# Attention and a feed-forward product on one core: VectorE's and GpSimd's two-operand SBUF operations planned apart, the softmax constant as an immediate

## The chip, the cores and the metric

The kernel runs on one core of one Trainium2 chip. The metric is device time in microseconds of one execution. TensorE (PE) multiplies matrices, with its weight loads (PEld) beside them; VectorE (DVE), ScalarE (ACT) and GpSimd (POOL) work on elements; SyncE (SP) issues nearly all DMAs. SBUF is the memory on the chip from which all of them read, PSUM the one into which PE writes its sums.

## The reference

```python
def _attn_ref(q, k, v):                     # q, k, v: 8 x 8 x 576 x 64
    ...
    scores = scale * np.matmul(q, k.transpose(0, 1, 3, 2))
    mask_local = (rel >= 0) & (rel < stride)              # stride 32, heads 0 to 3
    mask_strided = (rel >= 0) & (pos[None, :] % stride == pos[:, None] % stride)
    ...
    scores = scores - np.max(scores, axis=-1, keepdims=True)
    attn = np.exp(scores)
    attn = attn / (np.sum(attn, axis=-1, keepdims=True) + 1e-09)
    return np.matmul(attn, v).astype(np.float32)

def _moe_ref(x, w_in, w_out):               # x: 4608 x 512, w_in: 512 x 2048, w_out: 2048 x 512
    h = x @ w_in
    relu6 = np.clip(h + 3.0, 0.0, 6.0)
    g = h * relu6 / 6.0
    return (g @ w_out).astype(np.float32)
```

The output of the attention, heads side by side, is the x of the feed-forward part. All of it is float32.

## The kernel before

**Numbers in two parts.** A float32 operand of a large product is split into a high part (rounded to the format that PE takes, fp32r) and a low part (the rest, by a subtraction), and each product is done as three: high by high, high by low, low by high. So every weight tile, every x and every g needs a copy or cast for the high part and a subtraction for the low one. For x these are L430 on ACT and L433 on DVE; for g L887 on ACT and L890 on POOL.

**Weights.** Each of the 32 weight tiles is loaded raw by SP (L303) and put together from its bits: ACT takes the upper (L311) and the lower bits (L315), DVE joins them (L319, tiles `fi` and `fo` from `rawi` and `rawo`), ACT or POOL copies the high part (L327, L329, into `wi` or `wo`), and POOL or DVE subtracts for the low part (L337).

**Attention.** For each batch and pair of heads: PE turns q and k or DVE transposes them (L512, L529), PE makes the scores in PSUM (L597, L608), ACT or DVE copies them out as `e` (L619, L621), DVE finds the maximum (L631, L634), POOL subtracts it (L653, L638), ACT takes the exponential (L656, L641), DVE the sum (L659, L645). `inverse` adds 1e-9 from the tile `eps` (L663) and takes the reciprocal (L664), both on DVE. POOL multiplies (L668, L649), DVE transposes (L702, L708, L713, tiles `at`, `atloc`, `atkept`), and PE multiplies by v (L402, L746, L771, L787) into `pv`, from which x is split. The last 64 tokens of each batch go to `left` (L419, L421).

**Feed-forward.** Three batches (0, 1 and 2) run by themselves: for each of 16 chunks of the inner dimension, PE makes `ph` (L921 to L923), ACT applies the shifted relu (L956, tile `u`), DVE the gate (L960), ACT and POOL split g, and PE adds the second product into `acc` (L854 to L856). The weights arrive during the first of these, so it runs beside the weights' unpacking and the next batch's attention. The other batches (3 and 4, 5 and 6, 7 and the left tokens) run in three pairs, each with seven products of half size (L1094 to L1096) in place of eight, for which sums and differences of weights (L974, L984, L995, sent to memory and loaded again) and of x (L1033 and L1039, tiles `xc` and `hxf`) are made ahead, and results are put together from PSUM and the SBUF tile `htmp` (L1105, L1113). There the gate reads either `ph` in PSUM or `htmp` in SBUF.

**What sets the order.** No engine chooses at run time. Every operation is recorded in a `Plan` by `op`, with an engine (or several that could do it), a planned duration for each, what it reads and writes, and a due time. `emit` then goes through a simulated time: for each engine it takes the ready operation that can start first, by due time where several can, and of the engines the one whose operation starts earliest. The engine that gets it is fixed then, and each engine runs its operations in that order. An operation waits on its engine for those ahead of it whether it needs them or not. `emit` knows of DMA, of the fetch of PE's instructions, and of small matmuls that only fill PE's early gaps (`idle`); after 100 us of simulated time DVE waits `PATIENCE` (2 us) before it takes an operation that another engine could do too.

Of the kernel before, what the change touches and what calls it, by code (L numbers as in the profile page):

```python
# [20 lines left out]
P = 128  # L21
# [18 lines left out]
HIENG = {"ACT": 0.63, "POOL": 1.2}  # L40
# [22 lines left out]
PATIENCE = 2.0  # L63


class Plan:
# [12 lines left out]
    def op(self, engine, us, fn, reads=(), writes=(), due=0.0, room=0.0, mode="", after=0.0, take=None, give=None, early=0.0, words=6):  # L79
# [13 lines left out]
        self.ops.append((how, fn, before, due, room, mode, after, take, give, early, words))  # L93
        return n

    def emit(self, idle):
# [10 lines left out]
        mode, dma = "", 0.0  # L107
# [11 lines left out]
        while done < len(ops):  # L119
            done += 1  # L120
            best = None
            for e, r in ready.items():
                t0, first, kept = free[e], None, 0.0
                for due, n in sorted(r):
                    t = max(t0, avail[n] + (PATIENCE if e == "DVE" and avail[n] > WARM and len(ops[n][0]) > 1 else 0.0))
# [9 lines left out]
                if first is not None and (best is None or first[0] < best[0]):  # L135
                    best = (first[0], e, first[2])
            t, e, n = best
            how, fn, _, due, _, m, after, take, give, _, words = ops[n]
# [48 lines left out]
def attention_ffn(ctx: ExitStack, tc, q, k, v, w_in, w_out, out):  # L187
# [34 lines left out]
    eps = const.tile([P, 2, 8], F32, name="eps")  # L222
# [7 lines left out]
    def identity():  # L230
        nc.vector.memset(three, 3.0)
        nc.vector.memset(eps, 1.0e-9)
# [57 lines left out]
    def weight_part(k, w, g, i):  # L290
# [149 lines left out]
    def kept_pair(g):  # L440
# [220 lines left out]
        def inverse():  # L661
            x = st_of(1)
            nc.vector.tensor_tensor(out=x, in0=x, in1=eps[:n, :, :nblk], op=ALU.add)  # L663
# [5 lines left out]
        pool = 0.1 + 0.004 * cols  # L669
        red = 0.18 + 0.0019 * cols  # L670
        if shifted:
            for j in range(2):
                ej, sj = (ekey + "1", stkey + (1,)) if j else (ekey, stkey)
                op("DVE", 0.18 + 0.00095 * cols, partial(most_of, j), reads=[ej, stkey], writes=[sj], due=sd + 0.7)
                op("POOL", pool / 2 + 0.05, partial(less_of, j), reads=[sj], writes=[ej], due=sd + 1)
                op("ACT", 0.2 + 0.00085 * cols, partial(exp_of, j), writes=[ej], due=sd + 1.5)
        else:
            op("DVE", red, most, reads=[ekey, ekey + "1"], writes=[stkey], due=sd + 0.7)
            op("POOL", pool, less, reads=[stkey, ekey + "1"], writes=[ekey], due=sd + 1)
            op("ACT", 0.2 + 0.0017 * cols, exp, writes=[ekey], due=sd + 1.5)  # L680
        if shifted:
# [3 lines left out]
            for j in range(2):  # L685
                op("POOL", pool / 2 + 0.05, partial(norm_of, j), reads=[stkey], writes=[ekey + "1" if j else ekey], due=sd + 2.5)
        else:
            op("DVE", red, total, reads=[ekey, ekey + "1"], writes=[stkey], due=sd + 2)
            op("DVE", 0.4, inverse, writes=[stkey], due=sd + 2.1)
            op("POOL", pool, norm, reads=[stkey], writes=[ekey, ekey + "1"], due=sd + 2.5)  # L690
# [191 lines left out]
    def split_g(fc, uk, gk, due, t, held=False):  # L882
# [9 lines left out]
        op({"POOL": 1.35}, 0, lo, reads=[uk, gk[0]], writes=[gk[1]], due=due)  # L892
# [395 lines left out]
```

## Time and profile before

| | us |
|---|---|
| three runs | 929.01, 932.99, 928.42 |
| median | 929.01 |
| the profiled execution | 929.12 |
| its span, first to last instruction | 927.3 |
| PE busy in the span | 885.3 |

The mean granted clock of TensorE over the span is 0.978 of full speed. The page's slices show when each engine is busy: each digit is the share of a slice of 23.2 us in tenths.

```profile
PE   5789898999999999999999999999999999999997
DVE  3788866568766777466755723345457003323200
ACT  2656655333434435344444633444446234334421
POOL 3646765555765877222221955213139531112441
PEclk7579999999999999999999999999999999999999
```

PE is the engine that is nearly always busy; its gaps lie in the first slices. DVE, ACT and POOL are busiest in the first half, where softmax, the weights' unpacking and the sums for the pairs stand beside the products. A clock under 9 is in the first three slices.

### The profile page before, as it was taken

What the parts mean: (1) busy time and instruction counts of PE and PEld (TensorE: products, weight loads), DVE (VectorE), ACT (ScalarE), POOL (GpSimd) and SP (SyncE); (2) the same over time, 40 slices, a digit from 0 to 9 for tenths busy, and PEclk for the clock granted to TensorE, in tenths of its full rate; (3) what the DMA queues carried; (4) which work ended last, traced back from release to release, by engine and by line L of the source; (5) the groups of instructions that cost most, each with busy time, mean ns of one, the idle gap of its engine ahead of it and who ended that gap; (6) DMA issues with size and microseconds to landing.
All of it is one profiled execution on the core that took longest, in us unless ns stands there. A gap on an engine that the chain in (4) does not pass through costs nothing.

```text
span 927.3 us, 19470 instructions
## 1 busy us (share of the span) xinstructions
PE 885.3 (95%) x7747; PEld 711.9 (77%) x7747; DVE 488.8 (53%) x833; ACT 404.6 (44%) x736; POOL 428.6 (46%) x378
## 2 busy tenths in 40 slices
PE   5789898999999999999999999999999999999997
PEld 3668686776888788888788778888887887888786
DVE  3788866568766777466755723345457003323200
ACT  2656655333434435344444633444446234334421
POOL 3646765555765877222221955213139531112441
PEclk7579999999999999999999999999999999999999
DMA  9988999977688874799784687785745675555374
GB/s 161 236 251 206 249 236 333 282 177 190 181 197 242 209 189 112 205 260 230 218 209 149 194 257 196 238 210 192 227 156 211 200 236 185 194 192 188 120 213 137
DMA packets 229563, 191.71 MB, mean 207 GB/s; under 512 B 174944, under 2 KB 189280, under 8 KB 229472
## 3 DMA queue, kind: packets, MB, share of 16 engines
q1 hardware_dynamic: 226800, 189.35, 73.2%
q10 hardware_dynamic: 2672, 1.11, 0.6%
q8 instruction: 61, 1.00, 0.5%
q14 instruction: 30, 0.25, 0.1%
HBM read 157.91 MB, written 32.51 MB: 205 GB/s over the span
## 4 chain that ended last, share of the span: by engine, by line
PE 75%; POOL 6%; DMA 6%; DVE 5%; SPq 3%; issue 2%; ACT 2%; DVEq 0%; POOLq 0%; ACTq 0%
PE ph L1094 8%; PE ph L1095 7%; PE ph L1096 7%; PE acc L854 4%; PE acc L856 4%; PE acc L855 4%; PE ph L921 3%; PE ph L922 3%; PE ph L923 3%; PE ps L608 3%; DMA rawi<-in_moe_w_in_dram 3%; DMA qn<-in_q_dram 2%; POOL xc L1033 2%; PE acc2b L854 2%; PE acc2b L856 2%
## 5 line engine op out<-in xcount | busy, mean ns | idle before, releaser
L1113 DVE TENSOR_TENSOR htmp<-ph,htmp 128x512 f32<-128x512 f32 x72 | 49.7, 690 | 183.9 <-ACT htmp L1105 106.7
L1094 PE MATMUL ph<-xc,wi 128*128 128x512 f32 x336 | 133.4, 397 | 1.3 <-DVE htmp L1113 0.8
L1095 PE MATMUL ph<-xc,wi 128*128 128x512 f32 x336 | 131.1, 390 | 0.0
L1096 PE MATMUL ph<-xc,wi 128*128 128x512 f32 x336 | 130.9, 390 | 0.0
L890 POOL TENSOR_TENSOR g<-u,g 128x512 fp32r<-128x512 f32 x48 | 65.7, 1372 | 62.1 <-ACT g L887 50.1
L921 PE MATMUL ph<-x,wi 128*128 128x512 f32 x192 | 79.8, 415 | 7.9 <-DVE u L960 4.6
L922 PE MATMUL ph<-x,wi 128*128 128x512 f32 x192 | 76.8, 400 | 4.0 <-DVE x L433 2.6
L923 PE MATMUL ph<-x,wi 128*128 128x512 f32 x192 | 76.7, 399 | 0.8 <-POOL wi L337 0.8
L854 PE MATMUL acc<-wo,g 128*128 128x512 f32 x192 | 76.9, 401 | 0.0
L855 PE MATMUL acc<-wo,g 128*128 128x512 f32 x192 | 75.1, 391 | 1.5 <-issue 1.1
L1094 PEld LDWEIGHTS ph<-xc,wi 128*128 128x128 f32 x336 | 63.0, 188 | 17.2 <-DVE htmp L1113 2.0
L856 PE MATMUL acc<-wo,g 128*128 128x512 f32 x192 | 75.4, 392 | 0.2 <-POOL g L890 0.2
L1096 PEld LDWEIGHTS ph<-xc,wi 128*128 128x128 f32 x336 | 63.1, 188 | 13.4
L1095 PEld LDWEIGHTS ph<-xc,wi 128*128 128x128 f32 x336 | 63.1, 188 | 12.4
L708 DVE STREAM_TRANSPOSE atloc<-e 32x192 f32<-32x192 f32 x168 | 61.9, 369 | 15.9 <-POOL e L668 9.0
L1105 ACT COPY htmp<-ph 128x512 f32<-128x512 f32 x72 | 42.2, 587 | 50.0 <-PE ph L1096 48.1
L653 POOL TENSOR_TENSOR e<-e,st 128x288 f32<-128x288 f32 (+1 forms) x30 | 34.2, 1141 | 64.5 <-DVE st L631 64.4
L890 POOL TENSOR_TENSOR g12a<-u,g02a 128x512 fp32r<-128x512 f32 x16 | 20.6, 1289 | 83.4 <-ACT g02a L887 83.4
L956 ACT ACTIVATE u<-htmp,three 128x512 f32<-128x512 f32 x48 | 34.7, 723 | 44.5 <-DVE htmp L1113 44.5
L956 ACT ACTIVATE u<-ph,three 128x512 f32<-128x512 f32 x48 | 33.0, 688 | 44.2 <-PE ph L923 43.8
L960 DVE SCALAR_TENSOR_TENSOR u<-u,htmp 128x512 f32<-128x512 f32 x48 | 38.5, 802 | 22.9 <-ACT u L956 22.8
L890 POOL TENSOR_TENSOR g11a<-u,g01a 128x512 fp32r<-128x512 f32 x16 | 21.5, 1347 | 60.4 <-ACT g01a L887 52.2
(212 smaller groups left out, 2079.5 us busy)
## 6 DMA issues: line engine op xcount, KB each, us to landing
wo<-wod SPq DMA_DIRECT2D x128, 512.0 KB
wi<-wid SPq DMA_DIRECT2D x84, 512.0 KB
rawi<-in_moe_w_in_dram SPq DMA_DIRECT2D x16, 512.0 KB
rawo<-in_moe_w_out_dram SPq DMA_DIRECT2D x16, 512.0 KB
wod<-wo SPq DMA_DIRECT2D x16, 512.0 KB
wid<-st SPq DMA_DIRECT2D x64, 128.0 KB
qn<-in_q_dram SPq DMA_DIRECT2D x112, 72.0 KB
kn<-in_k_dram SPq DMA_DIRECT2D x112, 72.0 KB
```

What stands on the lines that cost most here:

```text
L708: nc.vector.transpose(at[PAD * (a + h):PAD * (a + h) + PAD, :, PAD * a:PAD * a + PAD], e[PAD * a:PAD * a + PAD, :, PAD * h:PAD * h + PAD])
L854: nc.tensor.matmul(acc, gh, woh, start=fc == 0, stop=False)
L855: nc.tensor.matmul(acc, gh, wol, start=False, stop=False)
L856: nc.tensor.matmul(acc, gl, woh, start=False, stop=end)
L890: on(e).tensor_tensor(out=to(1), in0=tiles[uk], in1=tiles[gk[0]].bitcast(F32), op=ALU.subtract)
L921: nc.tensor.matmul(ph, wih, xh, start=n_ == 0, stop=False)
L922: nc.tensor.matmul(ph, wih, xl, start=False, stop=False)
L923: nc.tensor.matmul(ph, wil, xh, start=False, stop=n_ == NCC - 1)
L956: nc.scalar.activation(make(), src(), AF.Relu, bias=three)
L1094: nc.tensor.matmul(ph, w[:, j, 0], x[:, 0], start=u in (0, 1, 3) and j == 0, stop=False, skip_group_check=u in (2, 4, 5, 6))
L1095: nc.tensor.matmul(ph, w[:, j, 0], x[:, 1], start=False, stop=False, skip_group_check=u in (2, 4, 5, 6))
L1096: nc.tensor.matmul(ph, w[:, j, 1], x[:, 0], start=False, stop=j == 1, skip_group_check=u in (2, 4, 5, 6))
```

## The change

An operation can be recorded with `port=True`. `emit` holds the time `port` at which the last such operation on DVE or POOL ends (less 0.13 us), and starts no further one on either before it. So the plan runs the marked operations of the two engines one after the other. Marked are the join of weight bits, the low part of weights, the softmax's subtraction and multiplication on POOL, the low part of g, the gate where it reads `htmp` (given by `give`), and the sums, differences and low parts for the pairs. Not marked are POOL's cast of the high part (L329), and DVE's low part of x, which reads PSUM.

DVE's 2 us of patience now hold only for unmarked operations; a marked one with a choice of engines goes at once. Where two engines could start at the same time, the one whose operation is due first comes first. Planned durations are set anew. And the sum's 1e-9 is added as an immediate (`tensor_scalar_add`), so that the tile `eps` and its memset go.

```diff
-HIENG = {"ACT": 0.63, "POOL": 1.2}
+HIENG = {"ACT": 0.63, "POOL": 0.62}
...
-PATIENCE = 2.0
+PATIENCE = {("DVE", False): 2.0, ("DVE", True): 0.0, ("POOL", True): 0.0}
+PORT = ("DVE", "POOL")
...
-                    t = max(t0, avail[n] + (PATIENCE if e == "DVE" and avail[n] > WARM and len(ops[n][0]) > 1 else 0.0))
+                    t = max(t0, avail[n] + (PATIENCE.get((e, ops[n][11]), 0.0) if avail[n] > WARM and len(ops[n][0]) > 1 else 0.0))
+                    if ops[n][11] and e in PORT:
+                        t = max(t, port)
...
-                if first is not None and (best is None or first[0] < best[0]):
-                    best = (first[0], e, first[2])
+                if first is not None and (best is None or first[:2] < best[3]):
+                    best = (first[0], e, first[2], first[:2])
...
+            if shared and e in PORT:
+                port = end - 0.13
...
-    eps = const.tile([P, 2, 8], F32, name="eps")
-        nc.vector.memset(eps, 1.0e-9)
...
-        op("DVE", 0.95, join, reads=[key], writes=[fkey], due=due - 3)
+        op("DVE", 0.69, join, reads=[key], writes=[fkey], due=due - 3, port=True)
-        op({"POOL": 1.4, "DVE": 0.75}, 0, lo, reads=[fkey, key], writes=[key + ("lo",), key], due=due - 1)
+        op({"POOL": 1.29, "DVE": 0.68}, 0, lo, reads=[fkey, key], writes=[key + ("lo",), key], due=due - 1, port=True)
...
-            nc.vector.tensor_tensor(out=x, in0=x, in1=eps[:n, :, :nblk], op=ALU.add)
+            nc.vector.tensor_scalar_add(x, x, 1.0e-9)
...
-        pool = 0.1 + 0.004 * cols
+        pool = 0.12 + 0.00355 * cols
...
-                op("POOL", pool / 2 + 0.05, partial(less_of, j), reads=[sj], writes=[ej], due=sd + 1)
+                op("POOL", pool / 2 + 0.05, partial(less_of, j), reads=[sj], writes=[ej], due=sd + 1, port=True)
...
-        op({"POOL": 1.35}, 0, lo, reads=[uk, gk[0]], writes=[gk[1]], due=due)
+        op({"POOL": 1.3}, 0, lo, reads=[uk, gk[0]], writes=[gk[1]], due=due, port=True)
...
-        op({"DVE": 0.69, "POOL": 1.4} if both else {"DVE": 0.69}, 0, gate, reads=reads, writes=[uk], give=give, due=due)
+        op({"DVE": 0.69, "POOL": 1.4} if both else {"DVE": 0.69}, 0, gate, reads=reads, writes=[uk], give=give, due=due, port=give is not None)
...
-                op({"POOL": 1.34, "DVE": 0.69}, 0, lo, reads=keys_of(*at), writes=[key(u)], due=due + 0.5 * j + 0.1 * u + 0.05)
+                op({"POOL": 1.3, "DVE": 0.69}, 0, lo, reads=keys_of(*at), writes=[key(u)], due=due + 0.5 * j + 0.1 * u + 0.05, port=True)
```

What an engine can do in place of another shifts too: POOL makes 20 of the 32 high parts of weights (16 before) and 25 of their low parts (22 before), DVE 15 of the 32 differences L984 (5 before) and 9 of the copies of scores out of PSUM (4 before). The lines of the file after the change stand three further on (L433 becomes L436), those of the weights' unpacking included.

The first place is DVE's order around the first batch's last x, the one for which PE stands still at 63.90 us. `x0_31` is the low part of x for the heads 6 and 7, made in two steps from two PSUM tiles `pv0_30` and `pv0_31`; `fi` and `fo` are joins, `wi` the low part of a weight. Before:

```order
L433 TENSOR_TENSOR x0_11_875<-pv0_11_811,x0_10_874 128x224
L319 SCALAR_TENSOR_TENSOR fo03_854<-fo03_854,rawo03_506 128x512
L319 SCALAR_TENSOR_TENSOR fi10_862<-fi10_862,rawi10_511 128x512
L319 SCALAR_TENSOR_TENSOR fi11_905<-fi11_905,rawi11_514 128x512
L433 TENSOR_TENSOR x0_31_941<-pv0_30_911,x0_30_940 128x4x4x16
L319 SCALAR_TENSOR_TENSOR fi12_931<-fi12_931,rawi12_520 128x512
L337 TENSOR_TENSOR wi10_944<-fi10_862,wi10_944 128x4x128
L433 TENSOR_TENSOR x0_31_941<-pv0_31_912,x0_30_940 128x4x4x16
L337 TENSOR_TENSOR wi12_963<-fi12_931,wi12_963 128x4x128
```

Now:

```order
L436 TENSOR_TENSOR x0_11_872<-pv0_11_810,x0_10_871 128x224
L322 SCALAR_TENSOR_TENSOR fi10_860<-fi10_860,rawi10_509 128x512
L322 SCALAR_TENSOR_TENSOR fi11_881<-fi11_881,rawi11_516 128x512
L322 SCALAR_TENSOR_TENSOR fi12_910<-fi12_910,rawi12_518 128x512
L340 TENSOR_TENSOR wi10_936<-fi10_860,wi10_936 128x4x128
L436 TENSOR_TENSOR x0_31_945<-pv0_30_912,x0_30_944 128x4x4x16
L424 COPY left3_86<-pv0_30_912 128x4x4x2
L340 TENSOR_TENSOR wi12_948<-fi12_910,wi12_948 128x4x128
L436 TENSOR_TENSOR x0_31_945<-pv0_31_913,x0_30_944 128x4x4x16
L322 SCALAR_TENSOR_TENSOR fi13_958<-fi13_958,rawi13_522 128x512
```

The join `fo03` is gone from here and the low part `wi10` has come ahead of the first step; between the two steps stand a copy to `left3` and a low part in place of a join and a low part.

The second place is DVE's order in the first batch's chunk 12, where PE waits at 149.11 us for the gate `u0_12`, which reads `ph` and so frees it for a next product. `st1_1` is a softmax sum, `atloc` are transposes (six each). Before:

```order
L663 TENSOR_TENSOR st1_1_1845<-st1_1_1845,eps_78 96x2x6
L664 RECIPROCAL st1_1_1845<-st1_1_1845 96x2x6
L319 SCALAR_TENSOR_TENSOR fi33_1923<-fi33_1923,rawi33_1350 128x512
L708 STREAM_TRANSPOSE atloc0_899<-e_98 32x6x32 x6
L708 STREAM_TRANSPOSE atloc1_907<-e_98 32x6x32 x6
L960 SCALAR_TENSOR_TENSOR u0_12_1982<-u0_12_1982,ph0_12_1873 128x512
L960 SCALAR_TENSOR_TENSOR u0_13_1994<-u0_13_1994,ph0_13_1917 128x512
L319 SCALAR_TENSOR_TENSOR fo30_1950<-fo30_1950,rawo30_1678 128x512
L319 SCALAR_TENSOR_TENSOR fo31_1999<-fo31_1999,rawo31_1568 128x512
```

Now:

```order
L666 TENSOR_SCALAR st1_1_1834<-st1_1_1834 96x2x6
L667 RECIPROCAL st1_1_1834<-st1_1_1834 96x2x6
L322 SCALAR_TENSOR_TENSOR fi32_1889<-fi32_1889,rawi32_1351 128x512
L532 STREAM_TRANSPOSE kplain_108<-kn2_2_1721 128x18x4x8
L340 TENSOR_TENSOR wi32_1914<-fi32_1889,wi32_1914 128x4x128
L711 STREAM_TRANSPOSE atloc0_905<-e_102 32x6x32 x6
L322 SCALAR_TENSOR_TENSOR fi33_1933<-fi33_1933,rawi33_1423 128x512
L711 STREAM_TRANSPOSE atloc1_931<-e_102 32x6x32 x6
L322 SCALAR_TENSOR_TENSOR fo30_1959<-fo30_1959,rawo30_1667 128x512
L963 SCALAR_TENSOR_TENSOR u0_12_1985<-u0_12_1985,ph0_12_1891 128x512
L963 SCALAR_TENSOR_TENSOR u0_13_2037<-u0_13_2037,ph0_13_1901 128x512
```

The two gates stood right behind the twelve transposes and ahead of the join `fo30`; now `fo30` comes ahead of them, and the low part `wi32` and the transpose `kplain` have come into the row ahead of the first six.

The third place is PE's order at the first pair's end, where PE waits at 531.61 us for `g10a_15`, the low part of the pair's last g. `ph1_` are products of the second pair, `acc0a_0` a sum of the first. Before:

```order
L1096 MATMUL ph1_0_0_6576<-xc1_0_6441,wi0_6435 128x512
L1094 MATMUL ph1_0_1_6584<-xc1_1_6454,wi0_6435 128x512
L1095 MATMUL ph1_0_1_6584<-xc1_1_6454,wi0_6435 128x512
L1096 MATMUL ph1_0_1_6584<-xc1_1_6454,wi0_6435 128x512
L854 MATMUL acc0a_0_5177<-wo15_6426,g00a_15_6573 128x512
L855 MATMUL acc0a_0_5177<-wo15_6426,g00a_15_6573 128x512
L856 MATMUL acc0a_0_5177<-wo15_6426,g10a_15_6590 128x512
```

Now:

```order
L1097 MATMUL ph1_0_0_6560<-xc1_2_6549,wi1_6469 128x512
L1098 MATMUL ph1_0_0_6560<-xc1_2_6549,wi1_6469 128x512
L1099 MATMUL ph1_0_0_6560<-xc1_2_6549,wi1_6469 128x512
L1097 MATMUL ph1_0_3_6615<-xc1_3_6475,wi1_6469 128x512
L1098 MATMUL ph1_0_3_6615<-xc1_3_6475,wi1_6469 128x512
L1099 MATMUL ph1_0_3_6615<-xc1_3_6475,wi1_6469 128x512
L1097 MATMUL ph1_0_3_6615<-xc1_3_6517,wi1_6469 128x512
L1098 MATMUL ph1_0_3_6615<-xc1_3_6517,wi1_6469 128x512
L1099 MATMUL ph1_0_3_6615<-xc1_3_6517,wi1_6469 128x512
L857 MATMUL acc0a_0_5174<-wo15_6425,g00a_15_6600 128x512
L858 MATMUL acc0a_0_5174<-wo15_6425,g00a_15_6600 128x512
L859 MATMUL acc0a_0_5174<-wo15_6425,g10a_15_6623 128x512
```

Nine matmuls of the second pair, which read `xc1_2` and `xc1_3`, stand now ahead of the sum that needs `g10a_15`, where before the sum came right after `ph1_0_1`.

More of the change, by code (lines that the diff above doesn't have):

```diff
@@ L77, in __init__, with op @@
         self.by = {}
-    def op(self, engine, us, fn, reads=(), writes=(), due=0.0, room=0.0, mode="", after=0.0, take=None, give=None, early=0.0, words=6):
+    def op(self, engine, us, fn, reads=(), writes=(), due=0.0, room=0.0, mode="", after=0.0, take=None, give=None, early=0.0, words=6, port=False):
         n = len(self.ops)
@@ L92, in op @@
         how = engine if isinstance(engine, dict) else {engine: us}
-        self.ops.append((how, fn, before, due, room, mode, after, take, give, early, words))
+        self.ops.append((how, fn, before, due, room, mode, after, take, give, early, words, port))
         return n
@@ L106, in emit @@
         slots = {}
-        mode, dma = "", 0.0
+        mode, dma, port = "", 0.0, 0.0
         held, turned = 0, 0.0
@@ L678, in kept_pair @@
             op("DVE", red, most, reads=[ekey, ekey + "1"], writes=[stkey], due=sd + 0.7)
-            op("POOL", pool, less, reads=[stkey, ekey + "1"], writes=[ekey], due=sd + 1)
+            op("POOL", pool, less, reads=[stkey, ekey + "1"], writes=[ekey], due=sd + 1, port=True)
             op("ACT", 0.2 + 0.0017 * cols, exp, writes=[ekey], due=sd + 1.5)
@@ L685, in kept_pair @@
             for j in range(2):
-                op("POOL", pool / 2 + 0.05, partial(norm_of, j), reads=[stkey], writes=[ekey + "1" if j else ekey], due=sd + 2.5)
+                op("POOL", pool / 2 + 0.05, partial(norm_of, j), reads=[stkey], writes=[ekey + "1" if j else ekey], due=sd + 2.5, port=True)
         else:
@@ L689, in kept_pair @@
             op("DVE", 0.4, inverse, writes=[stkey], due=sd + 2.1)
-            op("POOL", pool, norm, reads=[stkey], writes=[ekey, ekey + "1"], due=sd + 2.5)
+            op("POOL", pool, norm, reads=[stkey], writes=[ekey, ekey + "1"], due=sd + 2.5, port=True)
         vb = [slot(early) for _ in range(2)]
@@ L974, in whole @@
                     on(e).tensor_tensor(out=tiles[tk.key].rearrange("p (u x) -> p u x", u=FQ), in0=a, in1=d, op=ALU.add)
-                op({"POOL": 1.34, "DVE": 0.69}, 0, whole, reads=[key, key + ("lo",), "tmps"], writes=[tk], take=tk, due=due + kc, early=due)
+                op({"POOL": 1.3, "DVE": 0.69}, 0, whole, reads=[key, key + ("lo",), "tmps"], writes=[tk], take=tk, due=due + kc, early=due, port=True)
                 w.append(tk)
@@ L984, in mix @@
                     on(e).tensor_tensor(out=part(*to), in0=part(*a), in1=part(*d), op=how)
-                op({"POOL": 0.74, "DVE": 0.42}, 0, mix, reads=w, writes=[w[to[0]]], due=due + kc + 0.1)
+                op({"POOL": 0.74, "DVE": 0.42}, 0, mix, reads=w, writes=[w[to[0]]], due=due + kc + 0.1, port=True)
             for i, us in enumerate(((2, 3), (6, 4))):
@@ L1039, in go @@
                     on(e).tensor_tensor(out=src(*to), in0=src(*x), in1=src(*y), op=ALU.subtract)
-                op({"DVE": 0.69, "POOL": 1.34}, 0, go, reads=keys_of(*x) + keys_of(*y), writes=keys_of(*to), due=due + 0.5 * j)
+                op({"DVE": 0.69, "POOL": 1.34}, 0, go, reads=keys_of(*x) + keys_of(*y), writes=keys_of(*to), due=due + 0.5 * j, port=True)
             split(0, (0, 0))
```

6 lines of the change are left out of this document (3 added, 3 removed).

## The prediction

> **What bounds the kernel now.** I read the page's busy times first, then stretches of the span, then PE's waits, then the groups by form and the timeline around the largest waits.
>
> ```profile
> span 927.3 us, 19470 instructions
> PE 885.3 (95%) x7747; PEld 711.9 (77%) x7747; DVE 488.8 (53%) x833; ACT 404.6 (44%) x736; POOL 428.6 (46%) x378
> ```
>
> TensorE sets the end: it is busy for 885.3 of 927.3 us, so all its idle time is 42.0 us. The change takes no matmul away and shortens none. It can win only out of these 42 us, and out of time in which PE ran at a lowered clock. VectorE and GpSimd are half idle: what they gain in busy time is worth nothing by itself.
>
> ```profile
> 0.00:20.00 20.00, 13.21 (x221) 8.00 (x222) 8.76 (x17) 4.89 (x9) 7.23 (x30) 0.74 1.11 156
> 20.00:40.00 20.00, 14.17 (x244) 12.35 (x245) 13.73 (x35) 10.47 (x24) 12.06 (x13) 0.55 1.06 206
> 40.00:60.00 20.00, 16.31 (x286) 13.49 (x283) 15.27 (x36) 12.91 (x28) 12.47 (x16) 0.85 0.98 287
> 60.00:80.00 20.00, 17.37 (x187) 13.47 (x185) 16.45 (x20) 12.95 (x26) 11.06 (x10) 0.83 0.74 194
> 80.00:100.00 20.00, 20.00 (x233) 16.00 (x231) 15.39 (x26) 10.94 (x22) 11.51 (x10) 1.00 1.00 253
> 100.00:225.00 125.00, 114.42 (x1216) 89.56 (x1215) 90.45 (x160) 59.19 (x111) 73.94 (x61) 1.00 0.90 244
> 300.00:500.00 200.00, 199.78 (x2075) 161.08 (x2075) 134.62 (x241) 89.58 (x170) 88.38 (x74) 1.00 0.76 199
> 500.00:720.00 220.00, 215.50 (x1448) 174.66 (x1448) 105.40 (x151) 100.36 (x176) 102.96 (x76) 1.00 0.68 208
> ```
>
> Columns: stretch, its length, busy time of PE, PEld, DVE, ACT, POOL, the granted clock, the DMA share. PE idles 6.8, 5.8, 3.7 and 2.6 us in the first four stretches (18.9 together), 10.6 from 100 to 225, 4.5 from 500 to 720, and nearly nothing between. The clock is below full only in the first 80 us.
>
> ```profile
> PE qp L498 <- DMA qn<-in_q_dram: 5.2, 3, 2.5
> PE ps L608 <- issue: 5.1, 2, 4.3
> PE ph L921 <- DVE u L960: 4.6, 4, 2.2
> PE ph L921 <- POOL e L653: 3.2, 1, 3.2
> PE ph L922 <- DVE x L433: 2.6, 1, 2.6
> ...
> PE acc0a L856 <- POOL g10a L890: 1.5, 1, 1.5
> ...
> PE ps L597 <- DVE x L433: 1.4, 1, 1.4
> ...
> PE acc1a L856 <- POOL g11a L890: 1.2, 1, 1.2
> ...
> PE ph L923 <- POOL wi L337: 0.8, 1, 0.8
> PE acc1b L856 <- POOL g11b L890: 0.7, 1, 0.7
> ...
> PE acc L855 <- POOL wo L337: 0.5, 1, 0.5
> PE ph L1094 <- DVE g L960: 0.4, 1, 0.4
> ```
>
> These are PE's waits: total, count, longest. DMA (5.2) and issue (5.1) are out of this change's reach. Those that VectorE or GpSimd release can move: 4.6 + 2.6 + 1.5 + 1.4 + 1.2 + 0.8 + 0.7 + 0.5 + 0.4 = 13.7 us. I leave the 3.2 out: the timeline shows a fetch of PE's instructions inside that wait.
>
> **The exclusion of DVE and POOL is in the trace.**
>
> ```profile
> L960 DVE SCALAR_TENSOR_TENSOR u<-u,htmp 128x512 f32<-128x512 f32 x48 | 38.5, 802 | 22.9 <-ACT u L956 22.8
> L960 DVE SCALAR_TENSOR_TENSOR u<-u,ph 128x512 f32<-128x512 f32 x48 | 32.5, 679 | 19.0 <-ACT u L956 16.6 <-POOL htmp L984 2.1
> L1033 DVE TENSOR_TENSOR xc<-hxf,xc 128x512 fp32r<-128x512 f32 x15 | 21.4, 1427 | 1.9 <-ACT xc L1030 1.8
> L890 POOL TENSOR_TENSOR g11b<-g,g01b 128x512 fp32r<-128x512 f32 x16 | 20.6, 1290 | 17.6 <-ACT g01b L887 17.6
> ```
>
> ```profile
> 529.83 1.72 POOL L890 TENSOR_TENSOR g10a<-u,g00a 128x512 fp32r<-128x512 f32 x1
> ```
>
> The gate takes 679 ns with one operand in PSUM and 802 with both in SBUF; the low part L1033, both in SBUF, takes 1427 on DVE. POOL's low part of g takes 1290 in one form, and 1.72 us at the place where PE waits 1.5 for it. I read the stretched ones as held up by the other engine's operation; term 1 shows two of them side by side with it. By the Trainium skill, SBUF — State Buffer, section "Who interferes with whom", a DVE instruction with two SBUF inputs excludes a GpSimd instruction that reads SBUF, and the second waits out the first; these rows agree. The old plan did not know of it, so what it put side by side came late. The new plan starts no marked operation until the other engine's is done, with durations near these rows (1.30 on POOL, 0.69 on DVE). That, the tie between engines decided by due time, and the dropped patience of DVE change only the order; they go together in terms 1 to 3. From some 730 us on PE's rows are the same before and after, and SP's first 60 rows are too, so the first loads and the end stay as they are.
>
> **Term 1: the wait at 63.90 us.**
>
> ```profile
> 57.09 0.68 DVE L319 SCALAR_TENSOR_TENSOR fo<-fo,rawo 128x512 int32<-128x512 int32 x1
> ...
> 59.86 1.80 DVE L319 SCALAR_TENSOR_TENSOR fi<-fi,rawi 128x512 int32<-128x512 int32 x1
> 61.59 1.75 DVE L337 TENSOR_TENSOR wi<-fi,wi 128x512 fp32r<-128x512 f32 x1
> 63.26 0.58 DVE L433 TENSOR_TENSOR x<-pv,x 128x256 fp32r<-128x256 f32 x1
> ```
>
> ```profile
> 59.83 1.29 POOL L337 TENSOR_TENSOR wo<-fo,wo 128x512 fp32r<-128x512 f32 x1
> 61.07 1.71 POOL L337 TENSOR_TENSOR wi<-fi,wi 128x512 fp32r<-128x512 f32 x1
> ```
>
> ```profile
> 63.90 0.80 PE L922 MATMUL ph<-x,wi 128*128 128x512 f32 x1 [2.63 <-DVE x L433]
> ```
>
> The low part of x at 63.26 is what PE waits 2.63 us for. Ahead of it on DVE stand a join of 1.80 and a low part of 1.75, each while a POOL operation ran; the same join took 0.68 at 57.09. So 1.12 + 1.07 = 2.19 us of the wait is exclusion. The new order has as much ahead of it (three joins, two low parts and a copy, against four joins and a low part), but planned apart from POOL. Bounds: nothing to all 2.63; I take 2.0, near the 2.19.
>
> After that wait the clock falls: the stretch 60 to 80 is granted 0.83, a loss of 0.17 x 20 = 3.4 us. Bounds 0 to 3.4; a wait of 2.2 us from 100 to 225 left the clock at 1.00 there, so a rest of under 1 us should leave it too. What the clock bears between 2.2 and 2.6 us no row says, so I take less than half: 1.5. By the Trainium skill, TensorE: Matmul & The Clock Gate, Part 1, a window of 3.4 us without enough work brings half rate, and it runs freely; with that rule all 3.4 or none would go. Term 1: 2.0 + 1.5 = **3.5 less**.
>
> **Term 2: 100 to 225 us.**The four waits for u (4.6), the other x (1.4), weights (0.8 + 0.5) are 7.3 us. The gates here have one PSUM operand and are not marked, but they stand in DVE's order behind joins (L319) that stretch. I take two thirds as gone: 4.9. Against it the order changes in both ways: at the longest of these waits (2.2) the new DVE order puts a low part and the join `fo30` ahead of the gate `u0_12`, which stood right behind the transposes before; the new PE order puts the next scores ahead of the product that waits. So I add two new waits of the mean size 4.6 / 4 = 1.15, rounded up for one longer one: 2.4. Bounds: all 7.3 gone, or 7.3 kept and 2.4 more. Term 2: 4.9 - 2.4 = **2.5 less**.
>
> **Term 3: 500 to 720 us.** Waits for POOL's g and DVE's gate: 1.5 + 1.2 + 0.7 + 0.4 = 3.8. At the first one, the new PE order puts nine ready matmuls ahead of the one that waits, and the low part it waits for had been stretched by 0.43 (1.72 against 1.29). What the others get I did not follow, so I take half as gone, 1.9, and one new wait of the mean size 3.8 / 4 = 0.95. Bounds 3.8 less to 0.95 more. Term 3: **0.95 less**.
>
> **Term 4: the immediate.**
>
> ```profile
> L663 DVE TENSOR_TENSOR st<-st,eps 128x16 f32<-128x16 f32 x16 | 6.6, 414 | 0.4
> L663 DVE TENSOR_TENSOR st<-st,eps 96x12 f32<-96x12 f32 x16 | 5.4, 339 | 0.4
> L664 DVE RECIPROCAL st<-st 128x16 f32<-128x16 f32 x16 | 4.0, 253 | 0.6
> L664 DVE RECIPROCAL st<-st 96x12 f32<-96x12 f32 x16 | 3.6, 225 | 0.5
> ```
>
> Thirty-two additions of 6.6 + 5.4 = 12.0 us. With one tensor less they should cost what the reciprocal on the same tile does (nearest row): 4.0 + 3.6 = 7.6, so 4.4 us of DVE. Ends: nothing saved, to the whole 12.0. On PE's path it is near nothing: no wait of PE names this line, and the steps behind (POOL's L668, the transposes) end in PE waits of 0.5 at most. The cover is PE's own matmuls of other products; without it each addition would save 0.14. Term 4: **0**. The Trainium skill (SBUF — State Buffer, "Who interferes with whom") speaks against it: tensor_scalar may enter a mode that takes the shared port as well, so POOL could still block it. No run here shows it; by that rule the busy time stays at 12.0, and term 4 still is 0.
>
> The lost memset of eps and one idle matmul fewer at the start: 0; the start waits for DMA.
>
> **Term 5: what comes late next.** From 80 to 100 the DMA share is 1.00, to 225 it is 0.90. A PE that is 4 to 6 us ahead meets loads of weights and of q and k that cannot come earlier. Ends: nothing, to all of terms 1 and 2 (6.0). PE's waits of that stretch name DVE, POOL and issue and no DMA, so I stay near the lower end with a sixth: **1.0 back**.
>
> **Term 6: the casts.**
>
> ```profile
> L329 POOL CAST wo<-fo 128x512 fp32r<-128x512 f32 x9 | 6.3, 700 | 12.8 <-DVE fo L319 11.3 <-ACT left L419 1.5
> ```
>
> POOL's high parts are planned at 0.62 now (1.2 before) but took 0.70, and they are not marked as excluding. Four more of them go to POOL (16 to 20): 4 x 0.70 = 2.8 us of POOL that ACT loses. Covered by POOL's idle half: 0; without that cover, up to the 2.8.
>
> Sum: -3.5 - 2.5 - 0.95 + 1.0 = -5.95. The span becomes 927.3 - 5.95 = 921.35. The profiled execution took 929.12, 1.82 around its span, so 923.2; it stands 0.11 above the median of 929.01. **923.1 us.**
>
> **Rivals.** *No difference.* The waits dissolve at one place and come back at the next in-order engine or at DMA: term 5 takes all 6.0 of terms 1 and 2. Then 929.1 - 0.95 = 928.2, and 926 to 931 around it. For it: PE is 95% busy, and from 225 to 500 has no idle to lose. Against it: the seven waits of term 2 are released by DVE or POOL, not by DMA.
>
> *Slower.* DVE used to hold back 2.0 us before it took an operation that POOL could take too; now it takes marked ones at once, and it runs in order. Between 100 and 225 a gate u whose ACT part is ready then stands behind a low part and a join more, as at `u0_12`. If the two are still stretched as at 59.86 and 61.59 us, that is 1.80 + 1.75 = 3.55 us; with 1.15 of it (the old mean wait) hidden by PE's other products, each such gate costs 2.4. It decides from two new ones on with the gains of the terms 1 to 3 not arriving: 929.1 + 2 x 2.4 = 933.9; with three, 936.3. I put 935 on it. For it: the order at `u0_12`. Against it: the plan prices these operations, and moves a gate back only where it holds PE to be busy.
>
> *The change does not do what it says.* The exclusion stays in fact, since planned and real starts drift apart and POOL's casts aren't marked. Then only the shuffled order counts: 929 give or take 2. It shares the chance of no difference.
>
> **How the numbers follow.** About 0.5% (4.6 us) is what a measurement of this kernel can tell from no change. Forecast (terms as above, 915 to 926): 0.58, three quarters of it, 0.44, under 924.4, since it lies 1.3 under that and has its longer tail below. No difference, with the plan that does not hold: 0.26. Slower: 0.16. So faster by over 0.5% (under 924.4) 0.44, within 0.14 + 0.26 = 0.40, slower (over 933.7) 0.16. The range: below, the bounds of terms 1 to 3 together (2.6 + 3.4 + 7.3 + 3.8 = 17.1) would give 912, and a share of it 914; above, the slower case's 935. I set 914 to 934, which leaves 2 in 10 out, most of it above. The likeliest case's own range is 915 to 926.
>
> **What would show it.** Term 1: PE's wait for x L433 under 1 us and the clock of 60 to 80 above 0.83. Term 2: the waits for u below 4.6 in total. Term 3: g10a's wait gone. Exclusion: DVE's L1033 well under 1427 ns, L960 with htmp near 679. Term 4: L666 of the new file near 225 to 253. Term 5: new waits for DMA before 225 us. The forecast is wrong if PE's idle from 100 to 225 stays at 10 us or grows, or if its first 80 us lose to a new half-clock window.

## The result, and the profile after

The changed kernel takes 920.12 us (median of six runs, 917.41 to 924.41) against 929.52 (six runs of the kernel before, 927.68 to 932.99). The ratio is 0.9899, with a 95% interval of 0.9871 to 0.9928: 1.0% faster. 923.1 us had been forecast. The profiled execution has a span of 917.7 us, 9.6 less than before.

The head of its page:

```profile
span 917.7 us, 19477 instructions
PE 887.2 (97%) x7746; PEld 714.4 (78%) x7746; DVE 502.0 (55%) x850; ACT 399.8 (44%) x722; POOL 425.9 (46%) x374
```

PE's busy time is 1.9 us longer than before; its idle time has fallen from 42.0 to 30.5 us. So all of the gain is idle time, as it had to be. DVE is busy for 13 us more, not less.

The stretches of the changed kernel, with the columns as before (length, PE, PEld, DVE, ACT, POOL, granted clock, DMA share, GB/s):

```profile
0.00:20.00 20.00, 14.19 (x221) 8.61 (x222) 9.21 (x18) 4.95 (x9) 7.36 (x31) 1.00 1.08 166
20.00:40.00 20.00, 16.71 (x380) 14.53 (x380) 16.27 (x38) 13.08 (x28) 13.83 (x14) 0.52 1.05 226
40.00:60.00 20.00, 15.51 (x147) 12.05 (x147) 14.54 (x33) 11.39 (x23) 16.33 (x19) 0.80 0.97 281
60.00:80.00 20.00, 18.62 (x198) 15.14 (x199) 17.83 (x25) 11.19 (x20) 13.10 (x12) 0.91 0.79 223
...
100.00:225.00 125.00, 119.28 (x1241) 93.46 (x1241) 89.13 (x161) 57.43 (x106) 75.65 (x65) 0.99 0.91 246
...
300.00:500.00 200.00, 197.56 (x2086) 158.80 (x2084) 131.02 (x239) 86.31 (x164) 81.44 (x67) 0.99 0.74 195
500.00:720.00 220.00, 219.73 (x1448) 179.22 (x1445) 110.66 (x153) 101.52 (x178) 100.26 (x73) 1.00 0.71 213
```

Set against the rows of before, PE's idle time falls by 2.7 us in the first 60 us (16.3 to 13.6), by 1.2 from 60 to 80, by 4.9 from 100 to 225 (10.6 to 5.7) and by 4.2 from 500 to 720 (4.5 to 0.3). It grows by 2.2 from 300 to 500, where there had been next to none. Two of these falls are smaller than they look. From 0 to 20 the idle time falls by 1.0 because the same 221 matmuls took 1.0 us longer (14.19 against 13.21). And of the 1.2 from 60 to 80, 0.85 is a part of one wait that now lies ahead of 60 us.

PE's waits of the changed kernel (total, count, longest):

```profile
PE ph L924 <- DVE u L963: 5.4, 5, 2.3
PE ph L925 <- issue: 3.5, 1, 3.5
PE kp L501 <- DMA kn<-in_k_dram: 3.0, 2, 1.6
PE ps L611 <- issue: 2.9, 2, 2.3
PE ph L925 <- DVE x L436: 2.2, 1, 2.2
...
PE acc2a L859 <- POOL g12a L893: 0.9, 1, 0.9
PE ph L924 <- ACT wi L330: 0.7, 1, 0.7
PE qp L501 <- DMA qn<-in_q_dram: 0.6, 1, 0.6
PE ph L926 <- DVE wi L340: 0.5, 1, 0.5
PE pv L405 <- DMA vloc<-in_v_dram: 0.4, 2, 0.2
...
PE ps L600 <- DVE x L436: 0.3, 1, 0.3
```

The waits for `g10a`, `g11a` and `g11b` are gone. Those for weights are not: 0.7 + 0.5 = 1.2 us, now released by ACT and DVE, against 0.8 + 0.5 = 1.3, released by POOL. The wait for the first batch's x is still there (2.2, it was 2.6), and the waits for u are longer in sum (5.4 against 4.6): one of them, of 2.3 us, is new and lies in the stretch from 300 to 500. This is what stands on DVE ahead of that gate:

```profile
348.54 4.20 DVE L1042 TENSOR_TENSOR hxf<-hxf,hxf 128x512 f32<-128x512 f32 x1
```

And this is POOL beside it:

```profile
348.22 1.47 POOL L671 TENSOR_TENSOR e<-e,st 96x768 f32<-96x768 f32 x1 [2.47 <-DVE st L667]
349.66 1.29 POOL L1036 TENSOR_TENSOR xc<-hxf,xc 128x512 fp32r<-128x512 f32 x1
350.91 1.29 POOL L893 TENSOR_TENSOR g<-u,g 128x512 fp32r<-128x512 f32 x1
```

An operation planned at 0.69 us took 4.20: POOL went from one operation straight to the next, and DVE got its turn only when POOL had nothing ready. All four operations are marked, so the plan had kept them apart. Such a long hold is rare, as the last section shows.

That the locks have not gone is plain in the groups by form as well (busy us, mean ns, idle before):

```profile
L963 DVE SCALAR_TENSOR_TENSOR u<-u,htmp 128x512 f32<-128x512 f32 x48 | 39.3, 819 | 18.5 <-ACT u L959 18.3
L1036 DVE TENSOR_TENSOR xc<-hxf,xc 128x512 fp32r<-128x512 f32 x12 | 15.4, 1290 | 3.4 <-ACT xc L1033 3.1
L666 DVE TENSOR_SCALAR st<-st 96x12 f32<-96x12 f32 x16 | 7.1, 442 | 0.3
L666 DVE TENSOR_SCALAR st<-st 128x16 f32<-128x16 f32 x16 | 6.4, 400 | 0.5
```

The gate on `htmp` takes 819 ns (802 before), L1036 takes 1290 (1427 before), and the additions take 13.5 us where they took 12.0. The whole trace says the same. Take DVE's two-operand operations with both inputs in SBUF, the additions left out: they lie beside a TENSOR_TENSOR of POOL for 86.1 us in the kernel before (154 operations) and for 92.7 in the changed one (162). So the kernel is faster with at least as much overlap as before. The experiments had to say what, then, the change does.

### The profile page after: what moved, and what is told of

The parts are those of the page before. It is cut to its first block, busy times and chain, and to the rows that moved or that the text cites. A ratio compares the mean times of both kernels' runs of the same rounds, so it can differ in the third digit from the quotient of the medians.

```text
span 917.7 us, 19477 instructions
## 1 busy us (share of the span) xinstructions
PE 887.2 (97%) x7746; PEld 714.4 (78%) x7746; DVE 502.0 (55%) x850; ACT 399.8 (44%) x722; POOL 425.9 (46%) x374
## 4 chain that ended last, share of the span: by engine, by line
PE 82%; DVE 5%; DMA 5%; SPq 4%; issue 1%; ACT 1%; POOL 1%; DVEq 0%; ACTq 0%; POOLq 0%
PE ph L1097 8%; PE ph L1098 8%; PE ph L1099 8%; PE acc L857 4%; PE ph L924 4%; PE acc L858 4%; PE acc L859 4%; PE ph L926 4%; PE ph L925 4%; PE ps L611 3%; DMA rawi<-in_moe_w_in_dram 2%; PE pv L405 2%; PE acc0b L857 2%; PE acc1b L857 2%; PE acc2b L857 2%; PE acc2b L859 2%
## 5 line engine op out<-in xcount | busy, mean ns | idle before, releaser
L1098 PEld LDWEIGHTS ph<-xc,wi 128*128 128x128 f32 x336 | 63.1, 188 | 12.4
L924 PEld LDWEIGHTS ph<-x,wi 128*128 128x128 f32 x192 | 37.2, 194 | 17.2 <-DVE u L963 7.9
```

The lines of the kernel that those rows point to most:

```text
L924: nc.tensor.matmul(ph, wih, xh, start=n_ == 0, stop=False)
L1098: nc.tensor.matmul(ph, w[:, j, 0], x[:, 1], start=False, stop=False, skip_group_check=u in (2, 4, 5, 6))
```

## The experiments

At first the question was whether the plan's exclusion brings the gain, or the start (the changed kernel is 2.5 us ahead by PE's wait for x, at 61.38 in place of 63.90 us), or merely another order. Some parts can be tried by themselves: the immediate leaves every engine's order as it is, and the tie rule changes only the first 20 us.

**The immediate alone.**

```diff
-            nc.vector.tensor_tensor(out=x, in0=x, in1=eps[:n, :, :nblk], op=ALU.add)
+            nc.vector.tensor_scalar_add(x, x, 1.0e-9)
```

> The kernel before with the immediate addition alone (the tile eps and its memset gone); every engine's order is that of before. Both theories: the same time as before within 1 us (929.5), since the softmax's additions are off PE's path. They differ in the addition itself: if an immediate spares it the wait behind POOL, the two forms take about 250 and 225 ns as the reciprocals do, 7.6 us in all; if it is held up as before (the changed kernel shows 400 and 442), 12 to 13.5 us.

931.81 us, ratio 1.0021 (1.0004 to 1.0038). The additions:

```profile
L661 DVE TENSOR_SCALAR st<-st 128x16 f32<-128x16 f32 x16 | 6.6, 413 | 0.4
L661 DVE TENSOR_SCALAR st<-st 96x12 f32<-96x12 f32 x16 | 5.3, 330 | 0.4
L662 DVE RECIPROCAL st<-st 128x16 f32<-128x16 f32 x16 | 4.1, 253 | 0.6
L662 DVE RECIPROCAL st<-st 96x12 f32<-96x12 f32 x16 | 3.6, 225 | 0.5
```

11.9 us, against 12.0 with the tensor: nothing is saved. The addition with an immediate is held up as the one with two tensors was, while the reciprocal on the same tile is not. In this run's trace an addition takes 0.16 to 0.18 us where no POOL operation runs beside it and up to 1.26 where one does; the reciprocal takes 0.22 to 0.25 in both cases. The Trainium skill's sentence cited in the prediction (SBUF — State Buffer, "Who interferes with whom", on tensor_scalar) fits; that it is this mode which takes the port was not tried apart. The 0.2% to the slower side is smaller than what a kernel's own runs differ by, and I give it no cause.

**The tie rule alone, and the change without it** (the line of the diff on the kernel before, and taken back in the changed one).

```diff
-                if first is not None and (best is None or first[0] < best[0]):
+                if first is not None and (best is None or first[:2] < best[3]):
```

> The kernel before with the new rule for ties alone. It changes the order in the first 20 us only: the first k and the second k are turned ahead of the first q and the second q. Theory 'exclusion' (the plan's exclusion brings the gain): 929.5, no difference. Rival 'start' (the changed kernel is 2.5 us ahead by 61 us because the first scores start about 1 us earlier and the fetch of PE's instructions with them): 926.5 to 927.5, and the wait named issue at 23.94 us (4.26) shrinks to about 2.3.

929.80 us, ratio 1.0000 (0.9982 to 1.0017).

> The changed kernel with the old rule for ties; only the first 20 us change, back to the first q ahead of the first k. 'Exclusion': 920.1, no difference. 'Start': 922.5 to 923, with the lead at PE's wait for x (61 us) gone from 2.5 to about 0.

922.04 us, ratio 0.9913 (0.9892 to 0.9935), whose interval overlaps with the changed kernel's. By its time alone this second run stands nearer to "start" (922.5) than to "exclusion" (920.1). But "start" also expected the lead at PE's wait for x to go, and it stayed: the wait ends at 61.54 us there. So the tie rule does not carry the gain: without the rest it gives nothing, and without it most remains. The theory "start" falls.

What makes the 2.5 us at the start stays open. In part it can be the scatter of single executions. The kernel before and the one with the immediate alone have the same order on PE, and the wait ends at 63.90 and 65.62. The changed kernel and the one that keeps the patience (below) have the same order on PE up to 136 us, and it ends at 61.38 and 63.01. The clock of 1.00 in the changed kernel's row from 0 to 20 is no sign of a faster start: its first two products for k and q take 1.19 and 1.17 us, where the kernel with the tie rule alone, whose row says 0.74, shows 0.69 and 0.70.

**The change without the exclusion.**

```diff
-                port = end - 0.13
+                port = 0.0
```

> The changed kernel, its planned durations, patience and tie rule kept, but the plan no longer keeps marked operations of DVE and POOL apart; much of the order differs from about 60 us on. 'Exclusion': the gain behind the start is lost, 926 to 929, with more of PE's waits released by DVE or POOL than the changed kernel has. Rival 'order' (planned and real starts drift by more than the slack, the locks happen anyway, and the gain comes from the other edits and the order they happen to give): 918 to 923, and the time that DVE's and POOL's operations are stretched stays within 10% of the changed kernel's.

948.82 us, ratio 1.0194 (1.0169 to 1.0219): 29 us more than with the exclusion, and 19 more than before the change. Both expectations were wrong about the time. Exclusion matters more than the theory of that name had it, and the order that the other edits give is bad by itself. Yet what "order" expected of the locks came true by this measure: DVE's operations with two inputs in SBUF lie beside POOL's for 100.9 us, 9% more than in the changed kernel (92.7). The page's head and the waits:

```profile
PE 888.6 (94%) x7746; PEld 712.0 (75%) x7746; DVE 513.3 (54%) x867; ACT 402.1 (43%) x728; POOL 403.9 (43%) x351
```

```profile
PE ph L924 <- DVE u L963: 7.8, 5, 2.4
...
PE ph L924 <- POOL wi L332: 5.1, 1, 5.1
PE ph L1097 <- ACT htmp L1108: 3.7, 2, 2.0
...
PE acc0b L857 <- ACT htmp L869: 2.2, 1, 2.2
```

**Four corners.** The planner writes down when it means each matmul to start. That is no measurement, but it can be set against one. The kernel before had its last matmul planned at 905.4 us, the changed one at 905.8, and the one without exclusion at 906.3: three plans of one length, with measured medians of 929.5, 920.1 and 948.8. So I formed a new theory, "true plan": the exclusion does not shorten the plan, it makes the chip follow it. Four kernels cross exclusion, durations and patience (the 2 us that DVE waits before it takes an operation POOL could take).

Exclusion (and the immediate) with old durations, old patience and the old tie rule, against the changed kernel; the other durations go back as the join's does:

```diff
-PATIENCE = {("DVE", False): 2.0, ("DVE", True): 0.0, ("POOL", True): 0.0}
+PATIENCE = {("DVE", False): 2.0, ("DVE", True): 2.0, ("POOL", True): 0.0}
...
-        op("DVE", 0.69, join, reads=[key], writes=[fkey], due=due - 3, port=True)
+        op("DVE", 0.95, join, reads=[key], writes=[fkey], due=due - 3, port=True)
...
```

> The kernel before with the exclusion in the plan and the immediate, but the old planned durations, DVE's old patience of 2 us and the old tie rule. The plan itself writes down when it means the last matmul to start: 905.4 us for the kernel before, 905.8 for the changed one, 906.3 for the changed one without exclusion (measured medians 929.4, 920.1, 948.8), and 917.3 here. Theory 'true plan': with exclusion the time follows the plan at the changed kernel's distance (14.3), without it it does not; here 917.3 + 14.3 = 931.6, slower than before though the locks are planned for. Rival 'order luck' (each reshuffle draws its own waits, the plan's end tells nothing): anything from 918 to 940, most likely near 925 to 929.

928.10 us, ratio 0.9969 (0.9949 to 0.9989). "True plan" missed by 3.5 us: it had a kernel slower than before (931.6), and this one is 0.3% faster, where the rival had it most likely.

The new durations alone, on the kernel before (`HIENG`, the join, the low parts and the softmax's operations on POOL as in the change):

```diff
-HIENG = {"ACT": 0.63, "POOL": 1.2}
+HIENG = {"ACT": 0.63, "POOL": 0.62}
...
```

> The kernel before with the new planned durations alone (no exclusion, old patience and tie rule, no immediate). The plan ends at 903.2. 'True plan': the shorter durations leave no allowance for the locks, so the distance is the 24 of before to the 42.5 of the kernel without exclusion: 927 to 946, and above before (931 or more) most likely. 'Order luck': 918 to 940 with no preference; if the durations alone carried the gain, 920 to 922.

932.76 us, ratio 1.0024 (0.9999 to 1.0049). Both theories allow this.

The change with the old patience (the first pair of lines of the diff of the exclusion alone, and nothing else):

> The changed kernel with DVE's patience of 2 us kept for every operation that has a choice of engines. The plan ends at 913.7. 'True plan': 913.7 + 14.3 = 928.0, so that nearly all of the gain would be gone. Rival 'patience is a side matter' (as the prediction took it): 919 to 923.

926.14 us, ratio 0.9954 (0.9927 to 0.9980): 1.9 below "true plan" and outside the rival's 919 to 923. The head of its page:

```profile
PE 888.1 (96%) x7746; PEld 712.3 (77%) x7746; DVE 476.4 (51%) x829; ACT 399.7 (43%) x723; POOL 442.0 (48%) x394
```

The change with the old durations:

> The changed kernel with the old planned durations (the join at 0.95, POOL's high part at 1.2 and so on), exclusion and patience and tie rule new. The plan ends at 906.8. 'True plan': 906.8 + 14.3 = 921.1, the same as the changed kernel. Rival 'the durations carry it': 926 to 930.

921.35 us, ratio 0.9892 (0.9853 to 0.9930), as "true plan" had it (921.1) and outside the rival's 926 to 930.

The durations carry nothing that can be told from the scatter. The patience, which the prediction had among the edits that only change the order, is worth 6 to 7 us where there is exclusion: 926.1 to 920.1, and 928.1 to 921.4. So the last corner was due.

**Patience dropped without exclusion.** On the exclusion alone, against which it changes two lines:

```diff
-PATIENCE = {("DVE", False): 2.0, ("DVE", True): 2.0, ("POOL", True): 0.0}
+PATIENCE = {("DVE", False): 2.0, ("DVE", True): 0.0, ("POOL", True): 0.0}
...
-                port = end - 0.13
+                port = 0.0
```

> The kernel before with the immediate and with DVE's patience dropped for the marked operations, but no exclusion in the plan; old durations and tie rule. The plan ends at 905.9. Theory 'interaction' (to take an operation at once only pays where the plan knows that the other engine holds it up; so far patience cost 6 us with exclusion, and dropping it without exclusion cost 16): the distance grows as without exclusion, 35 to 43, so 940 to 949. Rival 'patience alone' (the 2 us were simply too long): 921 to 926.

946.45 us, ratio 1.0184 (1.0137 to 1.0231), inside the range of "interaction". Its head and its longest group of waits:

```profile
PE 893.3 (94%) x7747; PEld 715.7 (76%) x7747; DVE 519.3 (55%) x865; ACT 402.7 (43%) x733; POOL 399.9 (42%) x348
```

```profile
PE ph L924 <- DVE u L963: 13.7, 9, 2.9
```

Without patience DVE takes work from POOL at once: DVE is busy for 519 and 513 us in the two kernels without exclusion and patience, against 489 before. The gates stand behind that work, and PE waits nine times for them, for 13.7 us (4.6 before). Of the 18.0 us by which this profiled execution is longer than that of the kernel before, 10.0 are idle time. The other 8.0 are busy time of PE, at a mean granted clock of 0.970 against 0.978. With exclusion known, the plan drops the patience and still puts only 502 us on DVE.

| kernel | exclusion | patience | durations | planned last matmul | median | difference |
|---|---|---|---|---|---|---|
| before | no | kept | old | 905.4 | 929.5 | 24.1 |
| durations alone | no | kept | new | 903.2 | 932.8 | 29.6 |
| patience dropped alone | no | dropped | old | 905.9 | 946.5 | 40.6 |
| change without exclusion | no | dropped | new | 906.3 | 948.8 | 42.5 |
| exclusion alone | yes | kept | old | 917.3 | 928.1 | 10.8 |
| change, patience kept | yes | kept | new | 913.7 | 926.1 | 12.4 |
| change, old durations | yes | dropped | old | 906.8 | 921.4 | 14.6 |
| the change | yes | dropped | new | 905.8 | 920.1 | 14.3 |

The rows differ in the tie rule and the immediate too, which by themselves brought no gain (above). With exclusion the chip is 11 to 15 us behind the plan's last matmul, without it 24 to 43. What exclusion is worth can be read at four places: 29 and 25 us with the patience dropped (948.8 to 920.1, 946.5 to 921.4), 7 and 1 with it kept (932.8 to 926.1, 929.5 to 928.1). Exclusion with the patience kept makes the plan longer (917.3 and 913.7), and nearly all that truth gains is paid back in the plan. Dropping the patience brings the plan back to 906; only a plan that knows of the locks can afford it. Nor is the gain one order's luck. Six kernels have exclusion and dropped patience: two of this table, the one without the tie rule above, and those of the next three experiments. They have five different orders and end at 916 to 922 us.

That the chip follows a plan with exclusion more closely is what the differences show. It does not come from fewer locks: DVE's operations with two inputs in SBUF lie beside POOL's for 92.7 us in the changed kernel, 14.3 behind its plan, and for 76.3 in the one with the durations alone, 29.6 behind its plan.

**The additions left out.** In this kernel the 1e-9 is not added to the sums; the plan still prices it.

```diff
-            nc.vector.tensor_scalar_add(x, x, 1.0e-9)
```

> The changed kernel without the 32 additions of 1e-9 (every sum holds an exponential of 0, so it is 1 or more, where 1e-9 is less than half a step of float32); the plan still prices them, so all else stands in the same order. The changed kernel's 13.5 us of DVE go. If the additions are off PE's path, as the prediction took them: 919 to 921.5. If they delay the softmax's chain where PE waits: 915 to 918.

920.51 us, ratio 0.9899 (0.9868 to 0.9930): the same as the changed kernel, with the 13.5 us of additions gone and DVE's busy time 11.9 us shorter (490.1). The additions are off PE's path.

**More of the locks marked.**

```diff
-        op(HIENG, 0, hi, reads=[fkey], writes=[key], due=due - 2)
+        op(HIENG, 0, hi, reads=[fkey], writes=[key], due=due - 2, port=True)
...
-            op("DVE", 0.4, inverse, writes=[stkey], due=sd + 2.1)
+            op("DVE", 0.4, inverse, writes=[stkey], due=sd + 2.1, port=True)
...
-PATIENCE = {("DVE", False): 2.0, ("DVE", True): 0.0, ("POOL", True): 0.0}
+PATIENCE = {("DVE", False): 0.0, ("DVE", True): 0.0, ("POOL", True): 0.0}
```

> The changed kernel with POOL's casts of weights and DVE's softmax additions and reciprocals marked too, and DVE's patience dropped for unmarked ones as well. The plan ends at 905.8, as for the changed kernel. 'True plan': a plan that knows more of the locks is followed more closely, distance under 14.3: 914 to 919. Rival 'order': the marks add nothing and the reshuffle brings its own waits: 920 to 927.

920.19 us, ratio 0.9894 (0.9854 to 0.9934), 14.4 us behind its plan's 905.8: no closer than the changed kernel, so here "true plan" expected too much. Marking the casts and the additions brings nothing, and what the other 14 us consist of stays open.

**The additions left out, and the plan told.**

```diff
-            op("DVE", 0.4, inverse, writes=[stkey], due=sd + 2.1)
+            op("DVE", 0.24, inverse, writes=[stkey], due=sd + 2.1)
```

> The changed kernel without the additions of 1e-9, and with the plan pricing the rest of that step (the reciprocal) at 0.24 in place of 0.4 us. The plan ends at 903.7. 'True plan': 903.7 + 14.3 = 918.0. 'Order': 918 to 927.

916.30 us (913.59 to 917.61), ratio 0.9848 (0.9803 to 0.9893). Beside it on the same chip, the kernel without the additions but with the changed kernel's order ran 918.64 to 921.29. So this version is faster than that one, and by its median 3.8 us ahead of the changed kernel. What it gains over the one beside it can only be the order, since both leave the additions out. Its plan is 2.1 us shorter (903.7), and 916.30 lies nearer to "true plan" (918.0) than to most of what "order" allowed; one kernel can't show that the shorter plan is the reason. Its waits:

```profile
PE ph L924 <- DVE fo L322: 3.7, 1, 3.7
...
PE acc L858 <- POOL g L892: 3.1, 3, 1.6
PE ph L924 <- DVE x L436: 2.1, 1, 2.1
...
PE ph L923 <- DVE u L962: 0.8, 1, 0.8
```

The waits for u are down to 0.8 us; a join and POOL's g have come in their place.

## Why the prediction was right, and where it was not

**What bounds it:** right. PE's busy time stayed, and the gain came out of the 42.0 us of idle time.

**The forecast:** right in direction, and 920.1 lies in the likeliest case's range of 915 to 926. The size was missed by 3 us to the small side; between the two profiled executions 5.95 had been expected, and 9.6 came. The terms, one by one:

- Term 1 (the wait at 63.90 us, 3.5): mis-sized. The wait went from 2.63 only to 2.23. The low parts ahead of x are still stretched, at the same place:

```profile
59.13 1.69 DVE L340 TENSOR_TENSOR wi<-fi,wi 128x512 fp32r<-128x512 f32 x1
```

  So 0.4 of the expected 2.0 came at the wait. The 1.5 for the clock cannot be told: the stretch 60 to 80 rose from 0.83 to 0.91, but the kernel with the immediate alone, in the order of before and with a wait of 2.60, shows 0.91 too, and the one with the tie rule alone, with 2.63, shows 1.00. The prediction took it that a wait of 2.2 us leaves the clock alone; after the one of 2.23 at 61.38 the changed kernel shows 0.73 from 60 to 64 us and 0.85 from 64 to 68. What the start brought was in no term.
- Term 2 (100 to 225 us, 2.5): the size double, 4.9 us less idle, but only half of it by the mechanism that was forecast. The waits for u, x and weights fell from 7.3 to 4.6 in this stretch: 2.7, near the forecast. Another 2.6 came out of waits named issue, of which the kernel before had 3.2 here (two of them below, and 0.8 for `ps`) and the changed one 0.6; the prediction had put these out of the change's reach. 0.4 for DMA is new.

```profile
PE ph L922 <- issue: 1.3, 1, 1.3
...
PE acc L855 <- issue: 1.1, 1, 1.1
```

  How idle time splits between the two names is not fixed: with the tie rule alone the same stretch idles 10.9 us, with 7.4 for u and 0.6 for issue. The two new waits of 2.4 did not both come there: in this stretch PE still waits four times for u, for 3.1 us. One came elsewhere, at 358.95 us, of 2.34, in a stretch that no term covered; it costs the 2.2 us that the stretch lost, and with it the sign "below 4.6 in total" failed (5.4).
- Term 3 (500 to 720 us, 0.95): mis-sized. 4.2 of the 4.5 us of idle time went: all three waits for POOL's g dissolved, not half, and the one new wait did not come. It was the order and not shorter operations. The low parts for which PE had waited at `g10a` and `g11a` take 1.74 and 1.59 us now (1.72 and 1.71 before). At `g10a` 18 matmuls of the next pair stand between the last two sums, where it was 12, and ahead of the sum that waited at `g11b` 9 and 3, where it was 3 and 3. At `g11a` POOL now makes that low part ahead of one of `g11b` (700.38 and 701.94 us), where before it came behind it (708.53 and 707.27).
- Term 4 (the immediate, 0): right for the time, wrong for the busy time. The bound "nothing saved" held, not the reciprocal's duration that I took; the additions' 12.0 us became 13.5 in the changed kernel.
- Term 5 (what comes late next, 1.0 back): it was not DMA. The waits for DMA fell in sum (5.2 to 4.0), with 0.4 new from 100 to 225; what came back is the gate at 358.95.
- Term 6 (the casts, 0): right. The experiment that marks them brought nothing.

**The step that failed** is the one that said of exclusion with its durations, tie rule and patience that they "change only the order; they go together", and so gave them one price. The tie rule does nothing, the durations do nothing, and exclusion and patience do only together what the prediction expected of exclusion: each alone gives 0.3% or makes the kernel 1.8% slower. Dropping the patience was the very mechanism of the rival "slower". The rival was priced at 935; the kernels without exclusion show it at 946 to 949. What kept it away is what the prediction held against it: the plan prices these operations. It does, but only with the exclusion in it.

**The test that failed** is the one on exclusion. Stretched operations were to become short; L963 on `htmp` stayed at 819 ns, and the overlap with POOL did not shrink (86.1 and 92.7 us). A DVE operation that the plan starts when POOL's has ended is ready earlier on the chip, is issued, and sits in the lock for the time that the plan had it wait. Its end is what counts, and the plan now has that end. This reading is argued from the stretched forms and from the differences to the plan, not shown for each operation. It also says why rival three ("the change does not do what it says") was half right: the exclusion does not hold on the chip, and the gain came nonetheless, because it holds in the plan.

## What to carry to other kernels

In a kernel whose order is fixed by a plan, set the planned end against the measured one, and model first what makes them differ. Here the plan's truth was worth more than its length: the plan of the durations alone is the shortest of the eight (903.2), and its kernel took 932.8. A rule of thumb in such a planner (here, wait 2 us before taking the other engine's work) may stand in for a missing model; taken out before the model is there it costs 16 us, after it gains 6. And the busy time of an engine off the path, or how much its operations are stretched, does not say whether such a change has worked.

## What the runs showed of the hardware that was not expected

A DVE operation held up by POOL mostly gets its turn as soon as POOL's operation ends, even where POOL's next one follows directly. The prediction's lines show it: the join at 59.86 us runs between POOL's two low parts, and the second of these takes 1.71 in place of 1.29. By the Trainium skill (SBUF — State Buffer, "Who interferes with whom") the second one blocks until the first finishes; these agree. But DVE can also be passed over, as in the operation of 4.20 us. Take all places of the fourteen traces where a DVE operation with two inputs in SBUF started while one TENSOR_TENSOR of POOL ran and another followed directly. Behind POOL's subtraction or multiplication on `e` in the form 96x768, DVE was passed over in 23 of 33; behind all other operations of POOL in 5 of 544. Why this form differs stays open.

How long PE waits does not by itself say whether its clock falls. The kernel with the immediate alone has PE's order of before and the same wait for `u0_12`, 2.21 us (2.19 before). It is followed by a granted clock of 0.57 from 151 to 155 us; before, the rows around that wait show 1.00.

An addition of an immediate to a 96x12 tile can be as short as this in the changed kernel's timeline:

```profile
347.65 0.17 DVE L666 TENSOR_SCALAR st<-st 96x12 f32<-96x12 f32 x1
```

It took 442 ns in the mean of its sixteen, longer than the one with two tensors before (339), while the reciprocal right after it on the same tile did not suffer:

```profile
L667 DVE RECIPROCAL st<-st 96x12 f32<-96x12 f32 x16 | 3.6, 224 | 0.5
```
